# Attention and gated MLP in one kernel: query tiles shifted by 16 tokens, attention in row and column tiles, f32 loads on one queue

## The chip, the cores and the metric

The kernel runs on one core of one Trainium2 chip. The metric is the device time of one execution in microseconds (us). A time is the median of several runs; the profile is one run of them. The span in a profile is a little shorter than the time of its run (278.2 us and 279.86 us for the profiled run of the changed kernel). Engines are named as in the profile: PE is TensorE, DVE is VectorE, ACT is ScalarE, POOL is GpSimd, SP is SyncE, which here only issues transfers (DMAs).

## The reference, cut to what matters

Local attention with block summaries, then an MLP. Four batches of 768 tokens, eight heads of 64, bf16 arithmetic allowed.

```python
block, window = 32, 16
k_sum = k.reshape(B, H, 24, 32, 64).max(axis=3)      # one summary key per 32 tokens
v_sum = v.reshape(B, H, 24, 32, 64).mean(axis=3)
scores = concat([where(|i - j| < 16, scale * q @ k.T, -1e9),
                 scale * q @ k_sum.T + log(32)])
x = softmax(scores) @ concat([v, v_sum])             # to [3072, 512]
h = x @ w_in;  g = h * sigmoid(beta * h)             # 512 -> 2048
out = g @ w_out                                      # 2048 -> 512
```

## The kernel before

Heads are handled in pairs (g = 0..3). A tile of 64 queries sees its own keys, 16 neighbours on each side (the halo) and the 24 summary rows: together at most 128 rows, so one matmul gives the scores of a tile. For even and odd tiles (`par` 0 and 1) there are two key matrices `kw` and two value matrices `ve`, `vo`. Halo and summary rows of the *values* must move to other partitions, which only a DMA does here:

```python
def prep_v(b, g):                                    # block means, then four row transfers
    ...
    nc.sync.dma_start(out=vo[0:W, 1:], in_=ve[0:W, 1:])
    nc.sync.dma_start(out=ve[P - W:P, 0:nch], in_=vo[P - W:P, 0:nch])
    ...
    nc.sync.dma_start(out=ve[SUM[0]:SUM[0] + nb, 0:nch, 0:n], in_=src)
    last["vw"] = nc.sync.dma_start(out=vo[SUM[1]:SUM[1] + nb, 1:, 0:n], in_=src)
```

Both heads of a pair share one full 128x128 matmul. Queries stand in `q2` with zeros for the other head, and half of what the value matmul computes is thrown away:

```python
cv(out=q2[0:D, :, :, 0], in_=qv[0:D]);  cv(out=q2[D:P, :, :, 1], in_=qv[D:P])   # in rows_qk
nc.tensor.matmul(sv[:, kk, j], kw[:, par, m, :], q2[:, m, par], ...)            # scores, N = 128
nc.tensor.matmul(ov[:, m // TB, m % TB], a[:, m], vt[:, m], ...)                # values, N = 129
for hh in range(2):                                                             # norm, 64 partitions
    nc.vector.tensor_mul(out=x[par * QT:(par + 1) * QT, :, hh, :]..., in0=ov[lo:lo + D, :, :, lo:lo + D], ...)
```

Batch 0 comes as f32 from three queues (SP, ACT, POOL). Batches 1 to 3 come through POOL's queue, which casts to bf16 on the way, and are transposed by DMA. While the MLP of batch b runs on PE, attention of batch b+1 is slotted in by a table of positions: steps 0 to 15 are hidden-layer tiles (`h_ps`), steps 16 to 39 quarter tiles of the output (`o_ps`). Each engine has its own list of instructions, in the order in which the kernel issues them.

The softmax here doesn't subtract the row's maximum and nothing guards it: scores larger than these inputs give would overflow.

## Time and profile before

257.5 us (median of three runs, 256.3 to 257.7). Busy time by stage of the kernel before; the columns are the window and its length, then busy us (and instructions) of PE, PE's weight loads, DVE, ACT and POOL, the granted PE clock (the speed allowed to PE, 1.00 is full), the DMA share (it can exceed 1, as here) and GB/s. The stages are the start (attention of batch 0), then the MLPs of batches 0 to 3, the last with the output's tail:

```profile
0.00:38.62 38.62, 20.83 (x215) 16.27 (x216) 29.84 (x92) 21.12 (x27) 24.02 (x41) 0.96 0.65 163
38.62:110.64 72.02, 53.50 (x342) 29.53 (x341) 34.67 (x80) 30.30 (x36) 48.52 (x59) 0.91 1.84 174
110.64:158.84 48.20, 48.20 (x342) 28.48 (x342) 29.65 (x68) 26.80 (x31) 21.80 (x26) 1.00 1.39 134
158.84:207.23 48.39, 48.39 (x346) 28.78 (x344) 27.65 (x68) 27.50 (x32) 0.00 (x0) 1.00 0.42 93
207.23:252.60 45.37, 41.52 (x225) 21.74 (x222) 4.15 (x6) 16.18 (x18) 0.00 (x0) 0.99 0.11 41
```

PE is busy without a gap in the third and fourth stage. It loses about 18 us in the start and 18 us in the second stage. The list of what PE waited for (us in total, times, longest) says where:

```profile
PE pk L221 <- POOL k_nat L173: 9.9, 2, 8.7
PE s_ps L285 <- DVE q_122 L265: 5.9, 1, 5.9
PE s_ps L285 <- DVE q_124 L265: 4.1, 1, 4.1
PE vm_ps L197 <- DMA ve_127<-in_v_dram: 2.5, 2, 1.8
PE av_ps L306 <- DMA ve_127<-vm_133: 2.4, 1, 2.4
...
```

The copies into `q2` and the row transfers of summary values are there, as are the loads. In a PE-bound stage the chain of waits shows the unit of work, one half of a head pair (start, length, what; x gives the instructions):

```profile
187.56 0.35 PE av_ps L306 x6
187.91 0.34 PE s_ps L285 x6
188.25 1.73 PE o_ps L361 x8
```

That is 2.42 us for six value, six score and eight output matmuls.

### The profile page before, as it was taken

To read this page: it belongs to the slowest core of one execution; us is meant where nothing else is said; L and a number is where in the kernel's file an instruction comes from. 1 tells how busy PE (TensorE), PEld (TensorE's weight loads), DVE (VectorE), ACT (ScalarE), POOL (GpSimd) and SP (SyncE) were. 2 spreads that over 40 slices of the span, in tenths; PEclk is the share of its full clock that TensorE was granted. 3 is DMA by queue.
4 is the path that set the end of the run, shared out by engine and by line. 5 is a ranking of instruction groups with operands and counts; after the bars stand their busy time and mean duration, and the time that the engine had idled before them with its cause. 6 is when DMAs were issued, how large, how long until landed. Compare 5 with 4: busy or idle time off the path is not lost.

```text
span 252.6 us, 3955 instructions
## 1 busy us (share of the span) xinstructions
PE 212.5 (84%) x1465; PEld 124.8 (49%) x1465; DVE 126.0 (50%) x314; ACT 121.9 (48%) x143; POOL 94.3 (37%) x125
## 2 busy tenths in 40 slices
PE   0478668987079398779999999999999999999993
PEld 0357545643126154446665664566656546664441
DVE  6968960230593699416377874275567720001221
ACT  0669718765035143047668441766765328661000
POOL 8768065239999968318598000000000000000000
PEclk9999979999559979999999999999999999999999
DMA  6973449999999999999999325544213631000122
GB/s 190 352 231 58 71 71 200 197 182 144 160 157 138 173 184 173 179 193 125 166 179 164 90 75 130 126 95 96 60 56 86 107 102 42 0 3 33 50 83 83
DMA packets 104370, 31.60 MB, mean 125 GB/s; under 512 B 91088, under 2 KB 100896, under 8 KB 104352
## 3 DMA queue, kind: packets, MB, share of 16 engines
q0 software_dynamic: 61120, 12.85, 64.9%
q1 hardware_dynamic: 39328, 16.94, 31.1%
q10 hardware_dynamic: 3904, 1.57, 2.3%
q8 instruction: 11, 0.18, 0.3%
q14 instruction: 7, 0.06, 0.1%
HBM read 27.27 MB, written 6.29 MB: 133 GB/s over the span
## 4 chain that ended last, share of the span: by engine, by line
PE 58%; DMA 24%; DVE 8%; POOL 3%; SPq 2%; issue 1%; ACT 1%; ACTq 1%
PE o_ps L361 27%; PE h_ps L346 25%; DMA ve_127<-in_v_dram 7%; DMA hold_81<-in_k_dram 6%; DMA q_tr<-q_nat 5%; DMA ve_127<-vm_133 3%; PE av_ps L306 3%; PE s_ps L285 2%; DVE x_nat L315 2%; DMA xT<-x_nat 2%; PE vm_ps L197 1%; DVE km L257 1%; POOL w_out_sb L375 1%; DMA vo_128<-vm 1%; POOL w_in_sb L372 1%
## 5 line engine op out<-in xcount | busy, mean ns | idle before, releaser
L361 PE MATMUL o_ps<-w_out_sb,h_sb 128*128 128x512 bf16 x384 | 91.9, 390 | 1.7 <-DVE w_out_sb L163 1.7
L346 PE MATMUL h_ps<-xT,w_in_sb 128*128 128x384 bf16 x512 | 86.6, 328 | 2.8 <-DMA xT<-x_nat 1.7
L350 ACT ACTIVATE h_sb<-h_ps,beta_sb 128x768 bf16<-128x768 f32 x64 | 57.1, 901 | 24.0 <-PE h_ps L346 23.4
L346 PEld LDWEIGHTS <-w_in_sb 128*128 128x128 bf16 x512 | 49.9, 98 | 35.7 <-issue 4.0
L361 PEld LDWEIGHTS <-h_sb 128*128 128x128 bf16 x384 | 37.2, 100 | 42.4 <-issue 6.3
L287 ACT ACTIVATE attn<-s_ps,bias 128x768 bf16<-128x768 f32 x32 | 28.4, 902 | 19.8 <-PE s_ps L285 19.3
L315 DVE TENSOR_TENSOR x_nat<-av_ps,r 64x384 bf16<-64x384 f32 x64 | 35.5, 555 | 1.5
L365 ACT COPY o_sb<-o_ps 128x512 f32<-128x512 f32 x18 | 10.6, 586 | 36.4 <-PE o_ps L361 30.3
L187 POOL DMA_DIRECT2D k_nat<-in_k_dram x24 | 20.5, 866 | 15.2 <-DMA kw_118<-k_nat 7.4
L365 DVE COPY o_sb<-o_ps 128x512 f32<-128x512 f32 x6 | 4.2, 692 | 41.9 <-PE o_ps L361 41.9
L187 POOL DMA_DIRECT2D q_nat<-in_q_dram x24 | 20.0, 844 | 8.0 <-PE h_ps L346 2.3
L306 PEld LDWEIGHTS <-attn 128*128 128x128 bf16 x192 | 13.4, 100 | 11.6 <-DVE attn L293 3.7
L293 DVE TENSOR_TENSOR attn<-attn,band 128x768 bf16<-128x768 bf16 x24 | 15.2, 634 | 7.3 <-ACT attn L287 6.7
L187 POOL DMA_DIRECT2D ve_127<-in_v_dram x16 | 13.4, 855 | 4.0 <-DMA w_out_sb<-in_moe_w_out_dram 3.8
L254 DVE COPY kw_118<-kw_118 128x480 bf16<-128x480 bf16 x3 | 0.9, 299 | 25.2 <-DMA kw_118<-k_nat 25.2
L163 DVE TENSOR_SCALAR w_out_sb<-w_out_sb,inv_beta 128x512 bf16<-128x512 bf16 x16 | 6.0, 428 | 14.6 <-DMA w_out_sb<-in_moe_w_out_dram 14.6
L221 PE MATMUL pk<-identity,k_nat 128*128 128x128 bf16 x24 | 2.6, 262 | 11.8 <-POOL k_nat L173 9.9
L312 DVE RECIPROCAL r<-av_ps 128x6 f32<-128x6 f32 x32 | 6.2, 195 | 9.6 <-PE av_ps L306 9.2
L285 PE MATMUL s_ps<-q_122,kw_118 128*128 128x128 bf16 x48 | 5.4, 253 | 6.6 <-DVE q_122 L265 5.9
L197 PEld LDWEIGHTS <-A_avg 128*128 128x128 bf16 x96 | 6.7, 101 | 4.8 <-DMA ve_127<-in_v_dram 3.2
L285 PEld LDWEIGHTS <-kw_118 128*128 128x128 bf16 x48 | 4.2, 114 | 8.9 <-DVE kw_118 L261 5.1
L221 PEld LDWEIGHTS <-k_nat 128*128 128x128 bf16 x24 | 1.9, 115 | 12.2 <-POOL k_nat L173 10.1
(143 smaller groups left out, 201.0 us busy)
## 6 DMA issues: line engine op xcount, KB each, us to landing
out_dram<-o_sb SPq DMA_DIRECT2D x24, 256.0 KB
k_nat<-in_k_dram POOLq DMA_DIRECT2D x24, 96.0 KB, 6.8
q_nat<-in_q_dram POOLq DMA_DIRECT2D x24, 96.0 KB, 6.4
w_in_sb<-in_moe_w_in_dram POOLq DMA_DIRECT2D x4, 512.0 KB, 6.9
w_out_sb<-in_moe_w_out_dram POOLq DMA_DIRECT2D x4, 512.0 KB, 14.9
ve_127<-in_v_dram POOLq DMA_DIRECT2D x16, 96.0 KB, 6.6
hold_81<-in_k_dram ACTq DMA_DIRECT2D x2, 384.0 KB
hold_82<-in_q_dram SPq DMA_DIRECT2D x2, 384.0 KB
```

The source lines that it names most:

```text
L187: nc.gpsimd.dma_start(out=dst[:, :, h], in_=src[b, g, :, h])
L197: nc.tensor.matmul(vm_ps[:], A_avg[:, c, :], ve[:, c, 0:2 * D], start=(c == 0), stop=(c == nch - 1))
L285: nc.tensor.matmul(sv[:, kk, j], kw[:, par, m, :], q2[:, m, par], start=not on_pe, stop=not on_pe or j == TB - 1)
L287: nc.scalar.activation(out=a.rearrange("p (k j) h q -> p k (j h q)", k=2), in_=big[:, :, 0:w], func=ACTF.Exp, bias=bias[:, par:par + 1], s ...
L293: nc.vector.tensor_mul(out=a, in0=a, in1=band[:, par, None, None, :].to_broadcast([P, nch, 2, QT]))
L306: nc.tensor.matmul(ov[:, m // TB, m % TB], a[:, m], vt[:, m], start=True, stop=True)
L312: nc.vector.reciprocal(out=r[:], in_=ov[:, :, :, 2 * D])
L315: nc.vector.tensor_mul(out=x[par * QT:(par + 1) * QT, :, hh, :].rearrange("p (k j) d -> p k j d", k=2), in0=ov[lo:lo + D, :, :, lo:lo + D] ...
L346: nc.tensor.matmul(big[:, kk, 0:MG], w_in_sb[:, ki, ni * P:(ni + 1) * P], xT[b][:, ki, kk * MG:(kk + 1) * MG], start=(ki == 0), stop=(ki = ...
L350: nc.scalar.activation(out=h_bufs[(b, ni // 8)][:, ni % 8, :].rearrange("p (k m) -> p k m", k=2), in_=big[:, :, 0:MG], func=ACTF.Silu, sca ...
L361: nc.tensor.matmul(o_ps[:], h_bufs[(b, ni // 8)][:, ni % 8, ms * P:(ms + 1) * P], w_out_sb[:, ni, :], start=(ni == 0), stop=(ni == k2 - 1))
L365: (nc.scalar.copy if b + 1 < B else nc.vector.tensor_copy)(out=o_sb[:], in_=o_ps[:])
```

## The change

The intent: shift the query tiles by 16 tokens, so that a tile's keys are 96 or 64+32 rows of the same 128-row chunk, and put summaries at partitions 96 or 32. Then halo and summary rows of the values are already on the right partitions and the row transfers go. Each head gets its own tile of the PE array: scores contract over 64 rows (two row tiles), values have 64 stationary columns (two column tiles), so no zero-padded queries and no discarded half. All loads of queries, keys and values become plain f32 transfers on SP's queue; POOL casts later batches. Cut to its core, regrouped, cuts marked:

```diff
-        nc.sync.dma_start(out=vo[0:W, 1:], in_=ve[0:W, 1:])
-        nc.sync.dma_start(out=ve[P - W:P, 0:nch], in_=vo[P - W:P, 0:nch])
-        nc.sync.dma_start(out=ve[SUM[0]:SUM[0] + nb, 0:nch, 0:n], in_=src)
-        last["vw"] = nc.sync.dma_start(out=vo[SUM[1]:SUM[1] + nb, 1:, 0:n], in_=src)
+    def v_spread(b, g):                              # summary rows: same partitions, on POOL
+        ...
+            nc.gpsimd.tensor_copy(out=t[b % 2][lo:lo + SR, g, :, :, 0:D],
+                                  in_=vm[lo:lo + SR, None].to_broadcast([SR, nch, 2, D]))
 ...
+                        nc.tensor.matmul(sv[:, h, par, mi, lo:hi], kw[r, par, m, :], qt[r, t:t + hi - lo], ...
+                    nc.tensor.matmul(ov[par * QT:(par + 1) * QT, mi, h, 0:D + 1], a[:, h, par, mi], vt, ...
+        nc.vector.tensor_mul(out=x[:, hf * NH:(hf + 1) * NH], in0=ov[:, :, :, 0:D], ...      # 128 partitions
 ...
-    q_r, k_r = (a.rearrange("b (g h) (c p e) d -> b g p (h c) (e d)", p=P, h=2, e=NE) for a in (q, k))
+    q6_r, k6_r = (a.rearrange("b (g h) (p j) d -> b g p h j d", p=P, h=2) for a in (q, k))
+    def by_row(t):
+        return t.rearrange("p (j h d) -> p h j d", h=2, d=D)       # heads interleaved: 256-byte runs
+    for nm, g in (("k", 0), ("q", 0), ("k", 1), ("v", 0), ("q", 1), ("k", 2), ("v", 1), ("q", 2), ("k", 3), ("v", 2),
+                  ("q", 3), ("v", 3)):
+        load0(nm, g)                                               # all on nc.sync
 ...
+        scores(0, g, 0)                                            # batch 0, per pair
+        if g + 1 < npair:
+            rows_k(0, g + 1)
+        v_cast(0, g)
+        v_rows(0, g)
+        v_sum(0, g)
+        v_spread(0, g)
+        if g == 1:
+            load_w_in(0)
 ...
+    w_in_last = [load_w_in(i) for i in range(1, 4)][-1]            # after all four pairs
+    w_out_last = [load_w_out(i) for i in range(4)]
+            if g == 0 and nm == "k":
+                after(ins, w_in_last)                              # batch 1 loads wait for the weights
 ...
+                    if g >= 2:
+                        side += [(ca[g - 2] + 0.1, lambda g=g: [load_next(nxt, nm, g) for nm in "kqv"])]
+                side += [(k2 + 17.0 + 3.0 * g, lambda g=g: [load_next(nxt + 1, nm, g) for nm in "kqv"]) for g in range(2)]
```

Batch 0 is now transposed on PE in f32, batch 1 on PE in bf16, batches 2 and 3 still by DMA.

## The prediction

> **What bounds the kernel now.** The table of busy time by window splits the span of 252.6 us. (A) Attention of batch 0 until the hidden-layer matmuls run densely at 38.6 us: PE is mostly idle. (B) MLP of batch 0 with attention of batch 1, 38.6 to 110.6 us: 72 us. (C), (D): the next two batches, 48.2 and 48.4 us, PE busy throughout. (E) The last MLP, 41.5 us, then 3.8 us of output. C, D and E are PE-bound. In them the chain of waits shows, per head pair, 0.34 us of block sums, 2 x 0.34 of scores and 2 x 0.35 of values, 6.9 us per batch on top of 41.5. B should be about 48.4 and loses some 23 us. The list of PE's waits names the losses: 5.9 and 4.1 us for the expanded query copies (behind query transposes by DMA, 6.5 us each, behind casting loads from the GpSimd queue), 2.5 us for value loads, 2.4 us for summary rows moved by DMA (7.6 us in the chain), 1.7 us each for output weights and xT, and a lower clock after them (0.78 to 0.84 in 57 to 90 us). In A the last value rows come through a DMA, 2.3 us, and the weights are held behind it until 33.9 us.
>
> **What the change does.** It removes the row transfers and the zero-padded query copies (two DVE copies of 0.3 to 0.5 us per pair), and halves the normalisation multiplies: 64 of 64x384 at 555 ns become 32 of 128x384, at the same cost each: 18 us of DVE saved, mostly off the path. It moves the casts of later loads to GpSimd (0.84 us each now; 12 casts and 8 spreads, some 17 us per batch, fit in 48), and the loads to SP, in the order of use, the batch 1 loads behind weights. It adds f32 transposes on PE for batch 0 and bf16 transposes for batch 1 (48 x about 56 ns = 2.7 us).
>
> On PE the matmul count of scores and values doubles at half the width. The Trainium skill, "TensorEngine Tiling (Array Packing)", section Tiling Modes, says that independent tiles run in parallel but that changing the tiling mode drains the engine. Nothing in the trace of before shows either. I expect them to cancel: C and D stay at 48.5 us (47 to 51).
>
> **Sum.** A: about 34 us instead of 38.6 (first transposes at 5 to 6 us rather than 8.7, no DMA on the value path; each engine has 5 to 6 us of work per pair). B: 61 us instead of 72: 51 of PE work and about 10 of stalls, because the batch 1 loads now wait for the weights (7 MB in 22 us in the trace) while PE meets its transposes early in program order. C+D 97, E 41.5, tail 4.5. Span about 238; time 243 us, as the time lay 5 us above the span before.
>
> Predicted: 243 us, range 232 to 253; faster by over 2% 0.82, within 2% 0.13, slower 0.05.
>
> **What would show it.** Right: waits on query copies and on summary-row DMAs gone; dense hidden-layer matmuls from 31 to 37 us; stage B 56 to 66 us, with its longest PE waits at the batch 1 key and query transposes; C and D within 47 to 51.
>
> **What would make it wrong.** Mode drains of over 0.15 us per switch (8 per pair) would stretch C and D past 51. Slow f32 transposes (over 0.3 us each) or a slow single queue would push A past 40. Later weights or loads would stall B. If tiles overlap fully and loads arrive in time, C and D reach 46, B 52, and the time 228.

## The result, and the profile after

277.95 us (median of four runs, 277.1 to 279.9) against 257.6 for the kernel before in the same rounds: ratio 1.081, with a 95% interval of 1.076 to 1.087. Ratios in this document are the mean time of one kernel's fast runs over that of the other's of the same rounds, so not quite the ratio of the medians. The output is correct. The change costs 20 us where a gain of about 14.5 was forecast.

The same stages in the changed kernel:

```profile
0.00:48.63 48.63, 30.76 (x319) 21.84 (x320) 22.75 (x81) 21.62 (x28) 22.42 (x45) 1.00 0.67 118
48.63:123.83 75.20, 55.54 (x494) 30.58 (x493) 29.29 (x84) 32.76 (x40) 24.10 (x28) 0.89 0.92 170
123.83:176.50 52.67, 50.93 (x449) 27.19 (x449) 22.30 (x68) 26.82 (x32) 14.07 (x18) 0.96 0.74 139
176.50:232.10 55.60, 50.33 (x446) 26.96 (x446) 22.21 (x68) 24.95 (x30) 14.13 (x18) 0.97 0.66 135
232.10:278.20 46.10, 41.54 (x225) 21.74 (x222) 4.15 (x6) 16.18 (x18) 0.00 (x0) 1.00 0.12 41
```

Against before, the start is 10.0 us longer, the second stage 3.2, the third 4.5, the fourth 7.2 and the last 0.7. PE waits for other things than before:

```profile
PE pk L210 <- POOL k_nat L195: 11.4, 2, 10.9
PE h_ps L367 <- DMA xT<-x_nat: 9.0, 3, 6.9
PE vm_ps L268 <- DVE v_nat L248: 7.9, 4, 2.6
PE pk L210 <- DMA hold<-in_k_dram: 5.9, 2, 5.6
PE vm_ps L268 <- POOL v_nat L248: 5.3, 2, 3.8
...
```

The waits for query copies and row transfers are gone, as intended. In their place stand waits for the batch 1 keys (10.9 us at once), for the DMA transposes of the attention output (`xT`) at the end of stages, and for value casts. The unit of work in a PE-bound stage:

```profile
212.23 0.31 PE av_ps L331 x12
212.54 0.29 PE s_ps L303 x14
212.83 1.83 PE o_ps L382 x8
```

It lasts 2.43 us, as long as before: values and scores take 0.09 us less, the eight output matmuls 0.10 us more. DVE's normalisation multiplies fell from 64 of 555 ns to 32 of 557 ns (35.5 to 17.8 us in the costliest groups).

So the tiles and the multiplies did what they should. The time is lost in what waits for what, and in slower matmuls around these waits: PE's busy time, summed over the stages, rises from 212.5 to 229.1 us, 10 of these 16.6 us in the start, and the granted clock of the later stages is lower. (In run 9 below, with most waits gone, PE's busy time is 215.7 us.) The start of the changed kernel is one chain through three engines; this is its piece for one head pair, from the chain of waits:

```profile
18.95 1.49 PE pk L210 x6
20.46 0.81 ACT kw L213
21.29 0.95 DVE km L232
22.24 1.30 DVE kw L184 x5
23.54 0.48 DVE v_nat L248
24.07 0.82 PE vm_ps L268 x6
24.88 1.28 PE pq L210 x6
...
29.42 1.49 PE pk L210 x6
```

The lines left out are scores, the exponential, the transposed output of the pair before and the values, 3.3 us of work on PE and ACT one after the other. A pair takes 10.5 us (18.95 to 29.42). PE needs the block sums (`vm_ps`) of pair g next, these need the value cast (`v_nat`) on DVE, and DVE has the key rows of pair g+1 before it in its program, which wait for the key transposes just made. The values themselves have long been loaded. PE works at about half speed in all of this: the six matmuls of the block sums take 0.82 us and the six f32 transposes of the keys about 1.5 us, where a run below, on the same shapes, shows 0.51 and 0.88.

The row of GB/s over 40 equal slices (7 us each) of the changed kernel:

```profile
GB/s 147 222 217 97 75 2 64 204 191 212 222 221 99 38 81 143 248 223 201 179 142 2 104 81 212 227 236 225 155 12 68 106 84 87 2 0 0 78 77 75
```

The changed kernel never exceeds 250 GB/s (the kernel before has a slice of 352). Its transfers stop almost wholly around 35 to 42 us, while the weights wait in POOL's program for the last pair's summary rows.

### The profile page after: what moved, and what is told of

Same layout as the page of the kernel before. It is cut to its first block, busy times and chain, and to the rows that moved or that the text cites. A ratio compares the mean times of both kernels' runs of the same rounds, so it can differ in the third digit from the quotient of the medians.

```text
span 278.2 us, 4804 instructions
## 1 busy us (share of the span) xinstructions
PE 229.1 (82%) x1929; PEld 128.3 (46%) x1929; DVE 100.7 (36%) x307; ACT 122.3 (44%) x148; POOL 74.7 (27%) x106
## 4 chain that ended last, share of the span: by engine, by line
PE 59%; DMA 19%; DVE 6%; SPq 5%; ACT 4%; POOL 3%; issue 2%; POOLq 0%; ACTq 0%; DVEq 0%
PE o_ps L382 24%; PE h_ps L367 22%; DMA hold_n<-in_v_dram 5%; DMA hold_n<-in_k_dram 4%; DMA w_in_sb<-in_moe_w_in_dram 4%; DMA xT<-x_nat 4%; SPq L401 3%; PE av_ps L331 3%; PE s_ps L303 3%; PE vm_ps L268 2%; PE pk L210 2%; PE pq L210 2%; DVE km L232 2%; DMA hold<-in_k_dram 2%; DVE kw L184 1%
## 5 line engine op out<-in xcount | busy, mean ns | idle before, releaser
L232 DVE TENSOR_REDUCE km<-kw 128x24 bf16<-128x768 bf16 x16 | 15.2, 949 | 79.6 <-DMA kw<-k_nat 43.3
L305 ACT ACTIVATE attn<-s_ps 128x768 bf16<-128x768 f32 x32 | 25.7, 811 | 17.6 <-PE s_ps L303 17.4
L277 POOL COPY ve<-vm 32x768 bf16<-32x768 bf16 x16 | 15.0, 938 | 57.5 <-DVE vm L270 53.7
L268 PE MATMUL vm_ps<-v_nat,A_sum 128*128 128x128 bf16 x96 | 9.3, 242 | 13.1 <-DVE v_nat L248 7.9
L338 DVE TENSOR_TENSOR x_nat<-av_ps,r 128x384 bf16<-128x384 f32 x32 | 17.8, 557 | 1.1
L311 DVE TENSOR_TENSOR attn<-attn,band 128x768 bf16<-128x768 bf16 x24 | 14.0, 581 | 11.6 <-ACT attn L305 11.3
L331 PEld LDWEIGHTS <-attn 128*64 128x64 bf16 x384 | 9.4, 118 | 12.4 <-DVE attn L311 7.0
L331 PE MATMUL av_ps<-ve,attn 128*64 128x65 bf16 x192 | 12.8, 207 | 1.4 <-ACT xT L352 0.8
L277 POOL COPY vo<-vm 32x768 bf16<-32x768 bf16 x16 | 13.4, 837 | 0.8
L331 PE MATMUL av_ps<-vo,attn 128*64 128x65 bf16 x192 | 12.9, 207 | 0.0
L303 PE MATMUL s_ps<-qt,kw 64*128 64x64 bf16 (+2 forms) x416 | 12.3, 199 | 0.0
```

The source lines that it names most:

```text
L232: nc.vector.tensor_reduce(out=km[:, 0:nb], in_=kw[:, 0].rearrange("p m (n f) -> p (m n) f", f=block), op=ALU.max, axis=mybir.AxisListType.X)
L268: nc.tensor.matmul(vm_ps[:], A_sum[:, c], t[:, c], start=(c == 0), stop=(c == nch - 1))
L277: nc.gpsimd.tensor_copy(out=t[b % 2][lo:lo + SR, g, :, :, 0:D], in_=vm[lo:lo + SR, None].to_broadcast([SR, nch, 2, D]))
L303: nc.tensor.matmul(sv[:, h, par, mi, lo:hi], kw[r, par, m, :], qt[r, t:t + hi - lo], start=not on_pe, stop=not on_pe or end)
L305: nc.scalar.activation(out=a.rearrange("p h r m q -> p h (r m q)"), in_=big[:, :, 0:n], func=ACTF.Exp, scale=scale)
L311: nc.vector.tensor_mul(out=a, in0=a, in1=m[:, None].to_broadcast([P, 2, 2, NH * QT]))
```

## The experiments

Theory: the tiled attention is neutral on PE, and the time is lost to the order of things in three queues. (1) DVE's program order makes the start a chain. (2) The weights stand behind the last pair in POOL's program, and the batch 1 loads wait for the weights. (3) Loads for the batch after next stand before the last `xT` transpose in SP's queue. Rivals: slow f32 transposes and a cold PE in the start; the memory's rate; transposes that are slow by themselves; the one queue; costly changes of the array's tiling. Ratios are to the kernel before in the same rounds; the changed kernel's is 1.081.

| run | edit to the changed kernel | median us | ratio |
|---|---|---|---|
| 1 | value steps first | 267.9 | 1.040 |
| 2 | weights early | 265.5 | 1.024 |
| 3 | loads early | 269.1 | 1.037 |
| 4 | loads in another queue | 275.0 | 1.066 |
| 5 | 1, 2 and 3 | 260.2 | 1.011 |
| 6 | 1, 2, 3 and 12 buffers | 266.6 | 1.033 |
| 7 | wide runs | 273.8 | 1.064 |
| 8 | two queues | 286.8 | 1.118 |
| 9 | 1, 2, 3 and 7 | 248.5 | 0.968 |
| 10 | 1, 3 and 7 | 257.2 | 0.999 |
| 11 | 9, scores and values apart | 250.2 | 0.971 |

All outputs were correct. A median is of all four runs, a ratio of the fast ones alone. Runs 1, 4, 6 and 11 had one slow run of four, runs 2 and 3 two; so the ratio is the better measure there.

### 1. Value steps first

```diff
         scores(0, g, 0)
-        if g + 1 < npair:
-            rows_k(0, g + 1)
         v_cast(0, g)
         v_rows(0, g)
         v_sum(0, g)
         v_spread(0, g)
+        if g + 1 < npair:
+            rows_k(0, g + 1)
```

> Only the order on VectorE changes in batch 0: the value cast and the block-sum copy of pair g come before the key rows of pair g+1; the order on TensorE is the same. Theory (a serial chain through VectorE's program order makes the start long): the three waits of 2.57 us of TensorE for the value cast go, the dense hidden-layer matmuls start at about 40 us instead of 48.6, all later stages keep their length, and the time falls from 278 to about 270 us. Rival (f32 transposes and half-speed matmuls on TensorE are what makes the start long): start and time move by less than 2 us.

Measured: 267.9 us, the median of four runs of which three, 266.7 to 268.2, are fast. The fourth, the profiled one, fell in a slow state (439 us, every matmul slow), so the kernel was looked at once more:

> The same kernel as the first of these runs, whose profile fell in a state with all matmuls slow; one more look for a profile in the fast state. Dense hidden-layer matmuls from about 40 us, no wait of TensorE for the value cast of batch 0, time about 268 us.

That look took 268.4 us. The dense hidden-layer matmuls start at 36.0 us instead of 48.6, and PE's waits for the value cast in the start shrink from 7.9 to 2.1 us in all. Theory (1) holds for these 5.8 us. But the gain in the start, 12.6 us, is larger than that and than expected, and the trace of the look shows a second thing: from about 14 us on, its matmuls run at full speed (PE's timeline; the changed kernel takes 1.54 and 0.82 us for the first two of these groups and is slow until about 42 us):

```profile
15.93 0.88 PE L210 MATMUL pk<-identity,hold 128*128 128x128 f32 x6
18.44 0.51 PE L268 MATMUL vm_ps<-v_nat,A_sum 128*128 128x128 bf16 x6 [1.03 <-DVE v_nat L248]
36.04 8.29 PE L367 MATMUL h_ps<-xT,w_in_sb 128*128 128x384 bf16 x50 [0.89 <-ACT xT L352]
```

The slow execution, in which the matmuls stay slow throughout, hints at the shares: its start takes 41.5 us. By these single executions about 7 of the 12.6 us are the order and about 5.5 the faster matmuls. So the rival (slow matmuls) is not excluded; it is part of the answer, and the shares are not settled. Some of the gain came back: the first stall for batch 1 keys is 12.5 us there instead of 10.9. That the transposes are in f32 is not what makes the start long: in run 7, with bf16 transposes and faster loads but the old order, the dense matmuls still start at 45.4 us.

### 2. Weights early

```diff
         v_cast(0, g)
         v_rows(0, g)
+        if g == 1:
+            w_in_last = [load_w_in(i) for i in range(4)][-1]
+            w_out_last = [load_w_out(i) for i in range(4)]
         v_sum(0, g)
         v_spread(0, g)
-        if g == 1:
-            load_w_in(0)
 ...
-    w_in_last = [load_w_in(i) for i in range(1, 4)][-1]
-    w_out_last = [load_w_out(i) for i in range(4)]
```

> Only the place of the weight loads in GpSimd's program changes: all eight are issued at about 19 us, in GpSimd's idle time, instead of one at 27 and seven after 44 us. Theory (the late weights hold back the batch 1 loads, which wait for them): the last w_in lands by about 36 us instead of 55.7, the batch 1 keys land about 15 us earlier than 68.6, the 10.9 us stall of TensorE before the first batch 1 transpose falls under 3 us, and the time falls to about 268 us; the start may lengthen by up to 2 us as the weights share the DMA with the last batch 0 loads. Rival (the memory's rate is the limit, so the same bytes come as late): the stall shrinks by less than 4 us, or moves to the second pair.

Measured: 265.5 us, the ratio falls from 1.081 to 1.024 (two fast runs, 261.8 and 265.2 us; interval 1.014 to 1.035). The stall at the first batch 1 transposes is gone from the list of waits; what is left is 1.0 us at the second pair. Theory (2) holds. The rate of the memory was not the limit here, since the same bytes came in time once they were asked for in time.

### 3 and 4. Loads early, and loads in another queue

Run 3 changes the position only, run 4 the queue only:

```diff
-                side += [(k2 + 17.0 + 3.0 * g, lambda g=g: [load_next(nxt + 1, nm, g) for nm in "kqv"]) for g in range(2)]
+                side += [((26.0 if b == 0 else 12.0) + 2.0 * g, lambda g=g: [load_next(nxt + 1, nm, g) for nm in "kqv"]) for g in range(2)]
```

```diff
-                side += [(k2 + 17.0 + 3.0 * g, lambda g=g: [load_next(nxt + 1, nm, g) for nm in "kqv"]) for g in range(2)]
+                side += [(k2 + 17.0 + 3.0 * g, lambda g=g: [load_next(nxt + 1, nm, g, nc.gpsimd) for nm in "kqv"]) for g in range(2)]
```

> Only the place in SP's program of the loads for the batch after next changes: steps 26 and 28 (first stage) or 12 and 14 (later stages) instead of 33 and 36, so they no longer stand ahead of the last attention transposes. Theory (SP's queue is served in order, so the transposes of the last pair wait behind 2.4 MB of loads): TensorE's wait for xT falls from 9.0 to about 2 us, the wait for the value cast in the later stages from 5.3 to under 1 us, the third stage from 52.7 to about 48, the fourth from 55.6 to about 48, and the time to about 266 us. Rival (the transposes by DMA are slow by themselves, 4 to 5 us, and end the stage in any place): at most 3 us gained.

> The same loads stay at their steps 33 and 36 but are issued from GpSimd, so they stand in another queue but move the same bytes at the same time over the same engines. If the order in SP's queue is the cause: xT transposes are issued within 1 us of their x_nat, the wait for xT falls from 9.0 to 2 to 3 us, time about 270. If sharing the DMA engines is the cause, the transposes still land 4 to 6 us after their x_nat, the waits for xT stay above 6 us, and the time stays within 2 us of 278.

Run 3 gave 269.1 us: PE's wait for `xT` fell from 9.0 to 2.1 us. The stages of its profiled run are 49.7 us (third) and 53.5 us (fourth); the fourth keeps a wait of 3.0 us for a value cast, against the expectation. That profiled run counts as slow by its time, so only the waits are taken from it.

Run 4 gave 275.0 us. In the changed kernel the last `x_nat` of the second stage is ready at 113.2 us, but three loads are issued before its transpose, which lands 5.3 us after its issue (SP's queue in the timeline):

```profile
114.79 0.39 SPq L401 DMA_DIRECT2D hold_n<-in_k_dram  x1
115.30 0.74 SPq L401 DMA_DIRECT2D hold_n<-in_q_dram  x1
116.14 1.81 SPq L401 DMA_DIRECT2D hold_n<-in_v_dram  x1
118.48 2.15 SPq L346 DMA_TRANSPOSE xT<-x_nat  x1
```

In run 4 the same transpose is issued at once, and lands 15 us later (chain of waits):

```profile
109.14 0.57 DVE x_nat L338
109.71 0.02 issue
109.72 14.99 DMA xT<-x_nat
```

So my theory (3) was too narrow. The order in SP's queue does delay the transpose, but taking that order away gives the delay back as slower landing, most likely because the loads are in flight at the same time. The profile of run 4 is slow (granted clock 0.888), so the 15 us is a reading of one run; the timed fast runs point the same way. By their ratios run 4 gains some 4 us (two more than I allowed for this case) and run 3 some 11 us (two fast runs only, give or take 3). Of the two edits, asking for those bytes at another time is the one that helps most. That run 4 also puts the issuing of these loads into POOL's program was not tested apart.

### 5 and 6. All three, and all three with more buffers

Run 5 joins the three edits. Run 6 also loads all four pairs early, none in the stage that uses them:

```diff
-    hold_pool = ctx.enter_context(tc.tile_pool(name="hold", bufs=6))
+    hold_pool = ctx.enter_context(tc.tile_pool(name="hold", bufs=12))
-                    if g >= 2:
-                        side += [(ca[g - 2] + 0.1, lambda g=g: [load_next(nxt, nm, g) for nm in "kqv"])]
-                side += [((26.0 if b == 0 else 12.0) + 2.0 * g, lambda g=g: [...]) for g in range(2)]
+                side += [((26.0 if b == 0 else 12.0) + 2.0 * g, lambda g=g: [...]) for g in range(npair)]
```

> All three placements together: value steps before the key rows in batch 0, weights at about 19 us, loads of the batch after next early. They gained 10, 12.5 and 9 us alone. Theory (three separate causes, each an order in a queue): the gains add up but for some overlap of the first two, which both bring the weights forward: time 250 to 254 us, so 24 to 28 us below the changed kernel and 1 to 3% below the kernel before; start about 39 us, second stage about 58, third and fourth about 50. Rival (they cure the same wait): no better than 260 us.

> As the run with all three, and with 12 instead of 6 buffers for the f32 loads, so that all four pairs of the batch after next are loaded early (steps 26 to 32, or 12 to 18) and none inside the stage that uses them. Theory (what is left in the third and fourth stages is TensorE waiting for a value cast whose load was issued a few us before): the waits for the value cast in the later stages (4.3 us in the run with early loads) fall under 1 us, third and fourth stage at 48 to 49 us, 3 to 4 us less time than with all three. Rival (those waits are GpSimd's own in-order work): no change.

Both expectations missed. Run 5 gave 260.2 us (ratio 1.011, 1.001 to 1.021): the gains do not add up. Its dense hidden-layer matmuls start at 53.7 us, later than in any kernel above, and PE's waits from 15 to 54 us show why:

```profile
PE vm_ps L268 <- DVE v_nat L248: 6.8, 2, 5.4
PE av_ps L331 <- POOL ve L277: 4.8, 1, 4.8
PE pq L210 <- DMA hold<-in_q_dram: 4.5, 1, 4.5
...
```

Now that the start runs faster, the weights that are issued at 18 us meet loads of batch 0 that have not landed; the last queries and values come late (one load of values takes 24.5 us from issue to landing, against at most 5.8 us in the changed kernel). While PE waits for them, its granted clock falls (mean 0.57 from 25 to 50 us), so its matmuls are slow as well. The 4.8 us is POOL, issuing eight weight loads before the summary rows that PE waits for. Run 6 gave 266.6 us: the waits for value casts in later stages went, as expected, but with six more loads in front of it PE waits 11.1 us for the last `xT` of the second stage, the fault of the changed kernel in larger form.

### 7 and 8. Wide runs, and two queues

What was left was the rate of the loads. From 5 to 10 us almost only loads of batch 0 are in flight, and the kernel before moves far more (last column; before first, then after; in the next 5 us it is 356 and 216):

```profile
5.00:10.00 5.00, 1.29 (x12) 1.11 (x12) 4.43 (x16) 2.55 (x3) 5.00 (x7) 1.00 1.21 331
```

```profile
5.00:10.00 5.00, 3.83 (x16) 3.12 (x17) 3.06 (x12) 1.60 (x2) 0.00 (x0) 1.00 1.21 227
```

Two things differ: one queue instead of three, and 256-byte runs of queries and keys instead of 512, because the changed kernel interleaves the heads in the destination. The Trainium skill, "DMA: Bandwidth & Descriptors", section Specifications, gives 512 bytes as the smallest transfer at line rate; its section "Issuing engines are not separate DMA queues" says that all queues share the same 16 engines. Run 7 keeps the heads side by side (runs of 1536 bytes) and interleaves in a cast on POOL, so its batch 0 transposes are bf16; run 8 only shares the loads between SP and ACT:

```diff
     def by_row(t):
-        return t.rearrange("p (j h d) -> p h j d", h=2, d=D)
+        return t.rearrange("p (h j d) -> p h j d", h=2, d=D)
 ...
-        nc.gpsimd.tensor_copy(out=t.rearrange("p j h d -> p (j h d)"), in_=f)
+        nc.gpsimd.tensor_copy(out=t[:], in_=f.rearrange("p (h j d) -> p j h d", h=2, d=D))
 ...
+        if 1 <= g + 1 < npair:
+            cast6(0, "q", g + 1)                     # batch 0 too is cast before its transposes
+        if g + 2 < npair:
+            cast6(0, "k", g + 2)
```

```diff
-        load0(nm, g)
+        load0(nm, g, nc.sync if nm == "k" or (nm == "v" and g % 2) else nc.scalar)
```

> The changed kernel, with queries and keys of batches 0 and 1 loaded as runs of 1536 bytes per partition and head instead of 256 (heads side by side, not interleaved); the interleaving moves to a cast on GpSimd (0.83 us each), so that the batch 0 transposes become bf16. Same order of everything else. Theory (loads made of 256-byte packets run at about 220 GB/s here, so the loads themselves are slow): in the first 20 us the DMA moves 300 GB/s or more, batch 0 is in by about 16 us instead of 22, and the batch 1 keys and queries land 4 to 6 us sooner after the weights, so the 10.9 us stall falls to about 6; the start changes little, as it is a chain of engines: time 268 to 275. Rival (rate is set by the single queue): the rate stays near 220 GB/s.

> The changed kernel with the batch 0 loads shared between the SP and the ACT queue, same packets of 256 bytes. If one queue limits the rate: 300 GB/s or more in the first 15 us and the first transposes earlier than 5.6 us. If the packets do: about 220 GB/s as before, time within 2 us of 278.

The same window in run 7, then in run 8 (298 and 218 in the next 5 us):

```profile
5.00:10.00 5.00, 3.23 (x28) 2.08 (x30) 3.90 (x13) 2.32 (x3) 3.07 (x4) 1.00 1.08 311
```

```profile
5.00:10.00 5.00, 2.60 (x12) 2.42 (x12) 1.05 (x6) 0.00 (x0) 0.35 (x1) 1.00 1.36 221
```

Wider runs raise the rate, a second queue does not, which agrees with both sections of the skill. Not tested: the kernel before also used POOL's queue, so its comparison with the changed kernel is not of widths alone. Run 7 gave 273.8 us, within what was expected; the stall before the first batch 1 transposes fell from 10.9 to 3.2 us, with another 2.8 us at the first value cast of that batch. Run 8 gave 286.8 us, not the 278 expected: ACT spends its first 17.6 us issuing loads, and does its first work only then. PE waits 8.5 us for the first key copy on ACT. The change's choice of one queue on SP was the better one, for a reason that the rate does not show.

### 9 and 10. The four edits, and the same without early weights

> Value steps first, weights at about 18 us, loads of the batch after next early, and the runs of 1536 bytes. If in the run with all three the start grew to 53.7 us because weights and the last batch 0 loads shared a DMA that moved only 220 GB/s, the start is now about 38 to 42 us, the second stage about 57, third and fourth 50 each: time 242 to 250, faster than the kernel before. If the early weights still hold back the last queries and values, the start stays above 47 and the time above 253.

> As the run with four changes, but with the weights left where the change put them (one load at the second pair, the rest after the last pair). The start is about 36 us, as in the run with the value steps first, the second stage keeps a stall of 6 to 9 us at the first batch 1 transposes: second stage about 63, time 248 to 256. The difference to the run with four changes is what the early weights are worth once the start is short.

Run 9 took 248.5 us (248.4 to 250.0), a ratio of 0.968 with an interval of 0.963 to 0.973: faster than both kernels. Its first two stages (the others take 49.9, 51.9 and 46.5 us):

```profile
0.00:41.70 41.70, 23.69 (x320) 15.91 (x321) 24.31 (x81) 21.61 (x28) 30.75 (x55) 1.00 1.06 223
41.70:98.50 56.80, 53.10 (x494) 29.46 (x494) 28.55 (x84) 31.34 (x39) 22.80 (x25) 0.97 0.72 159
...
```

The start falls from 53.7 us (run 5) to 41.7 with the wide runs, which is what the reading of run 5 required (the edit also makes the batch 0 transposes bf16, and the two were not tried apart). It is still longer than the 38.6 us of the kernel before, with 3.2 us of waiting for summary rows that stand behind the weights in POOL's program; the gain over that kernel is the second stage, 56.8 us instead of 72.0. Run 10 took 257.2 us: its start is 37.9 us, but keys and values of batch 1 hold PE up for 4.7 and 1.9 us, and the second stage lasts to 105.6 us. By the medians, early weights are worth 8.7 us once the start is short.

### 11. Scores and values apart

```diff
-                side += [(t, lambda g=g, p=hf: scores(nxt, g, p)),
+                side += [(t - 1.0, lambda g=g, p=hf: scores(nxt, g, p)),
```

> The run with four changes, with the scores of the later batches one step earlier, so that scores and values of a half pair no longer stand side by side but each between two groups of four output matmuls. Same matmuls, twice as many changes between the 128x128 matmuls and the narrow ones. In the traces so far eight output matmuls take 1.83 us after narrow matmuls and 1.73 us after full ones. Theory (each return from narrow to full matmuls costs 0.1 us): a half pair takes 2.52 us instead of 2.42 in the fourth stage, four output matmuls after a narrow group 0.97 us and not 0.87, and the time grows by about 2 us to 250. Rival (the 0.1 us belongs to the output matmuls in this kernel, whatever stands beside them): a half pair stays at 2.42 us.

In the fourth stage the chain of waits now reads:

```profile
185.70 0.31 PE av_ps L330 x12
186.01 0.97 PE o_ps L381 x4
186.98 0.29 PE s_ps L302 x14
187.27 0.97 PE o_ps L381 x4
188.24 0.31 PE av_ps L330 x12
```

A half pair takes 2.54 us instead of 2.43, and each group of four output matmuls 0.97 us. Each return from narrow to full matmuls costs 0.10 us. The drain that the skill's tiling page names would look like this; so would a first weight load that is not hidden (one takes 98 ns on average at the output matmuls), and the runs do not tell the two apart. It is small, and in this kernel it cancels what the tiles save. The times (250.2 against 248.5) are in two sets of rounds whose intervals overlap, so the loss is read from the trace alone.

## Why the prediction was wrong

The span was to be 238 us and was 278.2. The terms of the sum, with what they measured:

| term | predicted | measured | missed by |
|---|---|---|---|
| start | 34 | 48.6 | 14.6 |
| second stage | 61 | 75.2 | 14.2 |
| third and fourth | 97 | 108.3 | 11.3 |
| last stage and tail | 46 | 46.1 | 0.1 |

**Start: the failed step is "each engine has 5 to 6 us of work per pair".** The work per engine was counted and the engines were taken to overlap. The count was right for DVE, ACT and POOL (5.4 to 5.7 us per pair by the stage's busy times) and too low for PE (7.7, at half speed). The overlap was wrong: the order in DVE's program makes a chain of 10.5 us per pair. Run 1 changes that order alone and shortens the start by 12.6 us, about 7 by the order and about 5.5 by matmuls that left their half speed, as far as single executions tell. What I named as the danger, f32 transposes above 0.3 us each, did not come: six take 1.28 to 1.53 us, 0.21 to 0.26 each. Half-speed matmuls were not foreseen.

**Second stage: the failed step is "about 10 of stalls, because the batch 1 loads now wait for the weights (7 MB in 22 us in the trace)".** That wait and its place were right, at 10.9 us. But PE stands still for 19.7 us of the stage, not 10: the stage ends in a 6.9 us wait for the last `xT`, behind and beside the loads of the batch after next (runs 3 and 4), which I had not seen. And "51 of PE work" measured 55.5, at a mean granted clock of 0.89 (0.83 in the 10 us before the first wait, 0.81 in the 10 us after it). That the start was late is not what made this stage long: in the look of run 1 the weights are issued 12 us earlier, from 32 us on, and the stage still takes 75.6 us. What takes the 10.9 us away is weights issued well before the end of the start (run 2); wider runs of the loads behind them shorten it (run 7).

**Third and fourth stage: "C and D stay at 48.5 us" was right for the half pair and wrong for the stages.** The half pair is 2.43 us against 2.42, and run 11 shows 0.10 us per return from narrow to full matmuls, so the cancelling that I expected is shown in size, whatever the 0.10 us consists of. But I took these stages as PE-bound without asking what the new placement of loads and casts would make them wait for: 1.7 us for `xT` at the end of the third, 1.5 and 3.8 us for value casts in the fourth. PE's work took 50.9 and 50.3 us in them instead of 48.2 and 48.4, with a granted clock of 0.65 in the 6 us after the 6.9 us wait and of 0.73 in the 6 us after the 3.8 us wait.

Right: waits for query copies and row transfers gone, multiplies at the same cost each, the last stage, the queue that carries loads in the order of use (run 8).

The prediction's picture of the change was not far from what the change can do: with four edits of order and layout (243 us were predicted), none of which touches the tiles, the time is 248.5 us. What it missed is that these orders were not in place.

Open: why the start's matmuls run at half speed in the changed kernel until about 42 us and only until about 16 us in the one before. Shorter waits alone do not decide it: with the order of run 1 they reached full speed at about 14 us in its look, but with the same order in run 10 only at about 30.

## What to carry to other kernels

Before crediting a rewrite with the work that it removes, walk through each engine's program in order and ask what stands ahead of the instruction that the busiest engine needs next; here moving one step on an engine that was 36% busy was worth 10 us. When a load's destination layout changes, look at the length of its contiguous runs first: 256 bytes instead of 1536 cost 27% of the rate here (227 against 311 GB/s), with the values left at 256 in both. Fixes of order interact, since a shorter stage meets loads that were early enough before, so test them together as well as alone.

## What the Trainium skill lacked or had wrong

- "TensorEngine Tiling (Array Packing)", Tiling Modes, says that changing the mode drains the engine but gives no cost. Here each return from 128x64 or 64x128 tiles to full matmuls costs 0.10 us (the drain or an unhidden weight load), and twelve to fourteen narrow matmuls take 0.28 to 0.31 us, against 0.34 to 0.35 for six full ones.
- "DMA: Bandwidth & Descriptors", Specifications, agrees with the runs, but the page has no measured rate for loads in runs of 256 bytes. Loads in 256-byte runs moved 216 to 227 GB/s; with queries and keys in 1536-byte runs and values still in 256, 298 to 311.
- The same page, "Issuing engines are not separate DMA queues", says that the sequencer time saved by sharing issues is usually small. In run 8 it is the other way round and large: loads on ACT's queue kept ACT from its first work for 17.6 us.
- "TensorE: Matmul & The Clock Gate", part 1, describes a half-speed state of a PE that has not been busy. The start agrees with it (0.82 us for six matmuls that take 0.51 in the look of run 1), but the granted clock in the profile reads 1.00 there, so that column does not show the state; in run 5, from 25 to 50 us, it does (mean 0.57). One execution, of run 1, had slow matmuls through its whole length, 439 us instead of 268, again with a granted clock of 1.0.
